# Four output accumulators instead of seven, a ring of 20 weight pairs, and a weight conversion in two steps

## The chip, the cores and the metric

The kernel runs on one core of a Trainium2 chip. The metric is the device time of one execution in microseconds (us). The engines of the core work side by side, each on its own list of instructions in order: TensorE (PE, matrix products), VectorE (DVE), ScalarE (ACT), GpSimd (POOL) and SyncE (SP, which issues all the DMAs here). They wait for one another through semaphores.

## What is computed

Causal attention with a decay gives x (2304 x 512). A gate and two layers follow:

```
logits = x @ w_gate;  P = exp(logits - logits.max())
for _ in range(8):                       # row, then column normalisation
    P /= P.sum(1, keepdims=True) + 1e-09
    P /= P.sum(0, keepdims=True) + 1e-09
    P *= N / E
for e in range(8):                       # 512 -> 1024 -> 512
    out += P[:, e:e+1] * (np.maximum(x @ w1[e], 0) @ w2[e])
h = out @ w_in                           # 512 -> 2048, w_in and w_out are float64
result = np.maximum(0.01 * h, h) @ w_out # 2048 -> 512
```

## The kernel before

**Products.** A fp32 product is made of three TensorE products, since each operand is held as a high and a low part (hi x hi, hi x lo, lo x hi). On top of that each 2 x 2 block product is done with seven products instead of eight (Strassen's form as Winograd wrote it), so its operands are blocks or sums of blocks. Such a product is 12 matmuls of 128 x 384 and takes 2.08 us.

**Units.** The tokens are cut into three parts of 768. The first layer has 16 groups of weights (two for each expert) and the second layer four, g = 16 to 19. A unit u is one group for one part. Part 0 skips the groups 0 to 3: their work is done in small steps ("fills") during the attention and at the start, into the tiles `acc`. So units 0 to 7 are the groups 0 to 3 of parts 1 and 2, units 8 to 43 the rest of the first layer, part by part within a group, and units 44 to 55 the second layer. In unit u's window TensorE does the seven products p1 to p7 of u (into h) and the seven products l1 to l7 of u - 1 (out of h), in the order p1 p2 l1 p6 l2 l6 p7 p5 l5 l7 p3 p4 l3 l4.

**What hangs on it.** From the p products ScalarE copies and VectorE adds the blocks of h (L1048, L1051, L1054) and applies the nonlinearity (L1065). GpSimd makes the sums S1 to S4 of them (L1074), ScalarE the high parts (L1079) and VectorE the low parts (L1083). The l products go to PSUM banks, and `evict` (L1092; L1090 where a sum begins) adds each to one of the part's seven accumulators, P2, C21, P53, P5, K, U2 and U3. Two banks of PSUM serve the l products, x and y. l6 writes the bank that held l1, so it waits for l1's eviction, "e l1"; likewise l5 waits for l2's. After the last group of a layer `x_add` (L1096) makes output blocks out of the accumulators, three additions for each part.

**Weights.** `w_make` splits a block of a group's two matrices (which = 0, first, and 1, second) into a pair of a high part (ScalarE, L161) and a low part (GpSimd, L162). `w_sum` (VectorE, L850) makes the sums of blocks, s0 to s3, in place; s0 comes after the pair 0 of the same matrix is made. There are 14 pairs, each in the place of its own position, and pair i of group g + 1 is made as soon as pair i of g has been used for the last time: those of the first matrix in the window of part 2, those of the second in the window after it.

**Conversion.** w_in and w_out come as float64. The `conv_*` functions turn them into fp32 in 64 pieces of 128 x 256: a load of 256 KB (L890), a square on ScalarE (L894), four operations on VectorE (L899 to L902) and a store (L903). A group of the second layer then loads its weights from there. Two pieces are done in each of the units 8 to 39.

**Operands.** The seven operands b11, b21, t2, t3, t1, b22 and t4 of a part (blocks and sums of blocks of x, high and low) are made once for each layer, go to DRAM, and come back for each product as loads of 768 KB into a ring of four (`xw`, L1014).

**Order.** It is written by hand: `at(time, key, name, function, need=...)` gives each step a planned time and the steps it needs. A step's time is raised to just after those it needs, and all steps are then written out sorted by time. Each engine takes its own in that order, so an instruction that waits holds up all behind it on its engine, and on SP all later DMAs.

```
    Q = "p1 p2 l1 p6 l2 l6 p7 p5 l5 l7 p3 p4 l3 l4".split()
    LACC = dict(l1="K", l6="U2", l7="U3", l4="C21", l5="P5", l3="P53", l2="P2")
        chain = {"l6": "l1", "l7": "l6", "l4": "l7", "l3": "l5", "l5": "l2"}
```

## Time and profile before

| | before |
|---|---|
| median of 3 runs | 2248.01 us (2247.16 to 2252.31) |
| the profiled execution | 2241.45 us |
| its span | 2239.3 us |
| TensorE busy in the span | 2066.7 us, 92% |
| VectorE | 1804.3 us, 81% |
| ScalarE | 1003.5 us, 45% |
| GpSimd | 1164.0 us, 52% |
| mean granted TensorE clock | 0.97 of full speed |

The profile is that of one execution, so times in it add up to 2241.45, not to the median. A wait of TensorE in it carries a "releaser": the step that ended it. Busy shares are means over the span; a stage by itself is read from the windows further down.

### The profile page before, as it was taken

To read this page: it belongs to the slowest core of one execution; us is meant where nothing else is said; L and a number is where in the kernel's file an instruction comes from. 1 tells how busy PE (TensorE), PEld (TensorE's weight loads), DVE (VectorE), ACT (ScalarE), POOL (GpSimd) and SP (SyncE) were. 2 spreads that over 40 slices of the span, in tenths; PEclk is the share of its full clock that TensorE was granted. 3 is DMA by queue.
4 is the path that set the end of the run, shared out by engine and by line. 5 is a ranking of instruction groups with operands and counts; after the bars stand their busy time and mean duration, and the time that the engine had idled before them with its cause. 6 is when DMAs were issued, how large, how long until landed. Compare 5 with 4: busy or idle time off the path is not lost.

```text
span 2239.3 us, 32628 instructions
## 1 busy us (share of the span) xinstructions
PE 2066.7 (92%) x11760; PEld 1996.0 (89%) x11760; DVE 1804.3 (81%) x2238; ACT 1003.5 (45%) x1802; POOL 1164.0 (52%) x728
## 2 busy tenths in 40 slices
...
GB/s 138 169 145 148 140 85 247 376 208 235 234 231 234 216 236 208 260 228 215 227 207 244 205 262 223 225 223 228 224 215 262 216 229 265 267 211 202 227 207 118
DMA packets 153512, 483.66 MB, mean 216 GB/s; under 512 B 16793, under 2 KB 42537, under 8 KB 153353
## 3 DMA queue, kind: packets, MB, share of 16 engines
...
HBM read 425.56 MB, written 51.22 MB: 213 GB/s over the span
## 4 chain that ended last, share of the span: by engine, by line
PE 49%; DVE 19%; issue 6%; POOL 5%; DMA 3%; ACT 2%; SPq 0%; DVEq 0%; POOLq 0%; ACTq 0%
PE x L1027 27%; PE y L1027 21%; DVE hl L1083 4%; DVE cv L899 2%; DVE cv L901 2%; DVE cv L900 2%; POOL wl L162 2%; POOL s L1074 2%; DMA xo_t<-stg 1%; DVE y L1051 1%; DVE u L1054 1%; ACT hh L1079 1%; DVE wr L850 1%; DVE acc_U L1092 1%; POOL k L1074 1%
## 5 line engine op out<-in xcount | busy, mean ns | idle before, releaser
L162 POOL TENSOR_TENSOR wl<-wr,wh 128x512 fp32r<-128x512 f32 x288 | 405.3, 1414 | 401.3 <-ACT wh L161 383.6
L1027 PE MATMUL x<-xw,wh 128*128 128x384 f32 x1792 | 467.1, 342 | 18.2 <-ACT k L1048 10.2
L1027 PE MATMUL x<-hh,wh 128*128 128x384 f32 x896 | 313.1, 349 | 75.5 <-DVE acc_K L1092 32.6
L1027 PE MATMUL y<-xw,wh 128*128 128x384 f32 x1344 | 350.8, 342 | 27.7 <-DVE u L1054 27.7
L1027 PEld LDWEIGHTS x<-xw,wh 128*128 128x128 f32 x1792 | 333.8, 194 | 21.7 <-ACT k L1048 11.1
L1027 PE MATMUL x<-hl,wh 128*128 128x384 f32 x896 | 309.0, 345 | 0.0
L1027 PE MATMUL x<-hh,wl 128*128 128x384 f32 x896 | 308.9, 345 | 0.0
L1027 PE MATMUL x<-xw,wl 128*128 128x384 f32 x896 | 303.9, 339 | 0.0
L1074 POOL TENSOR_TENSOR k<-k,u 128x768 f32<-128x768 f32 x56 | 103.3, 1845 | 366.2 <-DVE u L1065 282.6
L1027 PEld LDWEIGHTS y<-xw,wh 128*128 128x128 f32 x1344 | 246.7, 192 | 35.0 <-DVE u L1054 35.0
L1027 PEld LDWEIGHTS x<-hh,wh 128*128 128x128 f32 x896 | 173.7, 194 | 87.9 <-DVE acc_K L1092 40.7
L1027 PE MATMUL y<-xw,wl 128*128 128x384 f32 x672 | 229.4, 341 | 0.0
L1027 PE MATMUL y<-hh,wl 128*128 128x384 f32 x672 | 225.2, 335 | 0.0
L1027 PE MATMUL y<-hh,wh 128*128 128x384 f32 x672 | 225.2, 335 | 0.0
L1027 PE MATMUL y<-hl,wh 128*128 128x384 f32 x672 | 225.0, 335 | 0.0
L161 ACT ACTIVATE wh<-wr 128x512 fp32r<-128x512 f32 x288 | 177.5, 622 | 95.4 <-PE y L1027 58.3
L1079 ACT ACTIVATE hh<-c 128x768 fp32r<-128x768 f32 x112 | 94.5, 844 | 216.3 <-PE y L1027 104.7
L1048 ACT ACTIVATE u<-x 128x768 f32<-128x768 f32 x112 | 90.8, 811 | 217.8 <-DVE hl L1083 181.2
L1092 DVE TENSOR_TENSOR acc_P<-y,acc_P 128x768 f32<-128x768 f32 x138 | 131.4, 952 | 69.7 <-PE y L1027 69.4
L1079 ACT ACTIVATE hh<-u 128x768 fp32r<-128x768 f32 x112 | 94.9, 847 | 195.6 <-PE y L1027 104.3
L1027 PEld LDWEIGHTS x<-hh,wl 128*128 128x128 f32 x896 | 175.3, 196 | 0.0
L1027 PEld LDWEIGHTS x<-hl,wh 128*128 128x128 f32 x896 | 174.9, 195 | 0.0
...
## 6 DMA issues: line engine op xcount, KB each, us to landing
...
xw<-xo_b SPq DMA_DIRECT2D x168, 768.0 KB
...
```

Source lines behind the costliest of these rows:

```text
L161: nc.scalar.activation(hv, src, AF.Copy)
L162: nc.gpsimd.tensor_tensor(lv, src, f(hv), ALU.subtract)
L850: nc.vector.tensor_tensor(o, x, y, op)
L899: nc.vector.tensor_scalar(a, hi, 0x07FFFFFF, 3, ALU.bitwise_and, ALU.logical_shift_left)
L900: nc.vector.scalar_tensor_tensor(a, lo, 29, a, ALU.logical_shift_right, ALU.bitwise_or)
L901: nc.vector.scalar_tensor_tensor(a, hi, 0xC0000000, a, ALU.bitwise_and, ALU.bitwise_or)
L1027: nc.tensor.matmul(o_, w[:, k, w_], m[:, k, :], start=a and k + y == 0, stop=z and k == 1 and y == 2, skip_group_check=True)
L1048: nc.scalar.activation(ctile(u, name, name, bufs), pview(u, p), AF.Copy)
L1074: nc.gpsimd.tensor_tensor(tmp[u, o], tmp[u, a], tmp[u, b], op)
L1079: nc.scalar.activation(hi, tmp[u, LSRC[l]], AF.Copy)
L1083: nc.vector.tensor_tensor(lo, tmp[u, LSRC[l]], f(hi), ALU.subtract)
L1092: nc.vector.tensor_tensor(a, pview(u, l), a, ALU.add)
```

## The change

- The four accumulators of a part are the output blocks themselves, C11, C12, C21 and C22. l1 and l2 both go to C11, l6 and l3 to C12, l5 and l7 to C22, l4 to C21. The additions of `x_add` are no more. In a first group four evictions copy (ScalarE) and three add (VectorE), where all seven copied.
- The room goes to the weight pairs: one ring of 20, over all groups. Pair n takes the place of pair n - 20. So the first pair of a group's second matrix can be made once p2 of part 2 of the group before is done, and its first matrix's once that group's predecessor has done l2 of part 2. The steps are spread over the three windows of a group; the second matrix's mostly fall into the window of part 2.
- A conversion has a step a (two VectorE operations), the square on ScalarE, and a step b (two more, and the store), planned 6.1 us after a. Its two tiles are halves of the former `acc`. 40 pieces are done in units 9 to 41, one in each, and two in units 10, 15, 20, 25, 30, 35 and 40; 24 pieces are done in units 46 to 50, five in each and four in the last. a waits for the load on VectorE. The load is issued after step b of the piece two before.
- Part 0's operands for the first layer are made in units 5 to 8, one about every 13 us. At the start only part 2's and then part 1's are made.
- The last nine steps of the fills stand between unit 0's products (`f` in `QI`), and p1 and p2 of unit 0 take their operands from SBUF (`NEAR`). The transposes of `acc` into the accumulators move from units 0 and 1 to units 2 and 3. The transpose of the probabilities stands after p1 of unit 0.
- The last unit's sums S1 to S4 are on VectorE.

The core of the diff:

```diff
-XR = 4
+XR, WRING = 4, 20
...
-    wpa = pool("wpa", 4)
+    wpa = pool("wpa", 8)
...
-    wpc = pool("wpc", 3)
+    wpc = pool("wpc", WRING - 11)
...
-    ACC = ("P2", "C21", "P53", "P5", "K", "U2", "U3")
-    accp = []
-    for part in range(NPART):
-        own = ACC[:3] if part == 0 else ACC
-        accp.append({n: accs.tile([P, 2, TB], F32, name=f"acc_{n}_{part}") for n in own})
-    for x, n in enumerate(ACC[3:]):
+    ACC = ("C11", "C12", "C21", "C22")
+    accp = [{n: accs.tile([P, 2, TB], F32, name=f"acc_{n}_{part}")
+             for n in (ACC[:2] if part == 0 else ACC)} for part in range(NPART)]
+    for x, n in enumerate(ACC[2:]):
         accp[0][n] = half(acc_all[:, x * PT:(x + 1) * PT])
-    XPLACE = dict(b11="P2", b12="C21", b21="P53", b22="P5", t1="K", t2="U2", t3="U3", t4="C21")
+    spare = [accs.tile([P, 2, TB], F32, name=f"spare{x}") for x in range(3)]
+    spare += [half(acc_all[:, x * PT:(x + 1) * PT]) for x in (2, 3)]
...
-        pool_ = (wpc if i < 3 else wpa) if which == 0 else (wpa if i < 4 else wpb)
-        W[g, n] = w_split(blk(g, which, WSRC[which][n]), which, pool_)
+        x = (14 * g + 7 * which + i) % WRING
+        W[g, n] = w_split(blk(g, which, WSRC[which][n]), wpc if x < WRING - 11 else wpa if x < WRING - 3 else wpb)
...
+        t = spare[3 + j % 2].rearrange("p k t -> p (k t)")
+        wd = t[:, 0:2 * FH].bitcast(U32)
+        return wd, wd[:, 0::2], wd[:, 1::2], t[:, 2 * FH:3 * FH]
-    def conv_square(j):
-        wd, a, o = conv_tile(j)
-        nc.scalar.activation(o, f(wd[:, 1::2]), AF.Square)
-
-    def conv_bits(j):
-        wd, a, o = conv_tile(j)
-        lo, hi = wd[:, 0::2], wd[:, 1::2]
+    def conv_a(j):
+        _, lo, hi, o = conv_tile(j)
+        a = o.bitcast(U32)
         nc.vector.tensor_scalar(a, hi, 0x07FFFFFF, 3, ALU.bitwise_and, ALU.logical_shift_left)
         nc.vector.scalar_tensor_tensor(a, lo, 29, a, ALU.logical_shift_right, ALU.bitwise_or)
+
+    def conv_square(j):
+        _, lo, hi, o = conv_tile(j)
+        nc.scalar.activation(f(lo), f(hi), AF.Square)
+
+    def conv_b(j):
+        _, lo, hi, o = conv_tile(j)
+        a = o.bitcast(U32)
         nc.vector.scalar_tensor_tensor(a, hi, 0xC0000000, a, ALU.bitwise_and, ALU.bitwise_or)
-        nc.vector.scalar_tensor_tensor(o, o, TINY * TINY, f(a), ALU.is_ge, ALU.mult)
+        nc.vector.scalar_tensor_tensor(o, f(lo), TINY * TINY, o, ALU.is_ge, ALU.mult)
         nc.sync.dma_start(out=conv_src(j)[1], in_=o)
...
-        ps = pw["t"] = bank(ps1, "x1")[:, 0, :]
+        ps = pw["t"] = l2_bank()[:, 0, :]
...
-    INIT = dict(P2=(0, 0), P53=(0, 1), C21=(1, 0), P5=(1, 1))
+    INIT = dict(C11=(0, 0), C12=(0, 1), C21=(1, 0), C22=(1, 1))
...
-    QI = "p1 p2 p6 P2 p7 p5 P53 C21 p3 p4 P5".split()
+    QI = "p1 p2 f f p6 f f p7 p5 f f p3 f p4 f f".split()
...
-    LACC = dict(l1="K", l6="U2", l7="U3", l4="C21", l5="P5", l3="P53", l2="P2")
+    LACC = dict(l1="C11", l2="C11", l6="C12", l3="C12", l5="C22", l7="C22", l4="C21")
...
+    NEAR = ("p1", "p2")
...
-        nc.gpsimd.tensor_tensor(tmp[u, o], tmp[u, a], tmp[u, b], op)
+        (nc.vector if u == NU - 1 else nc.gpsimd).tensor_tensor(tmp[u, o], tmp[u, a], tmp[u, b], op)
...
-        new = g in (0, GE) or part == 0 and g == 4 and LACC[l] not in INIT
-        if new:
+        if g in (0, GE) and l in ("l1", "l6", "l5", "l4"):
             nc.scalar.activation(a, pview(u, l), AF.Copy)
         else:
             nc.vector.tensor_tensor(a, pview(u, l), a, ALU.add)
-    def x_add(stage, part, o, a, b, eng):
-        acc_ = accp[part]
-        eng.tensor_tensor(acc_[o], acc_[a], acc_[b], ALU.add)
...
+    for x, (dur, fns) in enumerate(fills[:nf - 9]):
...
+        xhi[0, 0] = {n: a[0] for n in XOPS}
+        xat[0, 0] = dict(b11=e[0], b12=e[1], t1=e[1], b22=e[0], t2=e[0], b21=e[1], t4=e[1], t3=e[2])
...
+    tp_ = base + 0.5
...
+    TURN = {(2, 0): "C11", (2, 1): "C12", (3, 0): "C21", (3, 1): "C22"}
...
+    t0 = unit0[4] + 2.0
+    st = (unit0[8] - 24.0 - t0) / 7
...
+        ta = t0 + st * x
+        for m, y in load:
+            at(ta - 6.0, X, f"load {n} {m}", lambda m=m, y=y: x_block(0, m, spare[y]), need=last)
+        ld = [(X, f"load {n} {m}") for m, _ in load]
+        if n[0] == "t":
+            at(ta, X, n, *((x_sum3,) if n == "t3" else (x_sum, 0, 0, n, nc.vector)), need=last + ld)
+            ld = [(X, n)]
+        at(ta + 1.1, X, "h " + n, x_hi, 0, 0, n, need=last + ld)
+        lo = spare[4] if n not in ("t4", "t3") else None
+        at(ta + 2.2, X, "l " + n, x_lo, 0, 0, n, nc.vector, lo, need=[(X, "h " + n)])
+        at(ta + 3.3, X, "o " + n, x_out, 0, 0, n, lo, need=[(X, "l " + n)])
+        last = [(X, "o " + n)]
...
+    U2 = keys.index((0, GE))
+    cu = []
+    for u in range(9, U2 - 2):
+        cu += [(u, 0)] + ([(u, 1)] if u % 5 == 0 else [])
+    for u in range(U2 + 2, U2 + 8):
+        cu += [(u, x) for x in range(5)]
+    for j, (u, x) in enumerate(cu[:64]):
+        C = ("cv", j)
+        ta = unit0[u] + (2.2, 8.4, 14.6, 20.0, 26.2)[x]
+        need = [(("cv", j - 2), "b")] if j > 1 else [(("x", 0, 0), "o " + n) for n in XOPS]
+        at(ta - 8.0, C, "load", conv_load, j, need=need)
+        at(ta, C, "a", conv_a, j, need=[(C, "load")])
+        at(ta + 2.0, C, "square", conv_square, j, need=[(C, "a")])
+        at(ta + 6.1, C, "b", conv_b, j, need=[(C, "square")])
...
+        g_, x = divmod(n - WRING, 14)
+        u_, name = keys.index((2, g_)), (PSEQ + LSEQ)[x]
+        return E_[u_, name] + 0.2, [(u_, name)]
...
+            t0, sp_ = unit0[us[0]] + 5.0, SL * len(us)
...
+                tf, need = w_free(14 * g + 7 * which + x)
+                ts.append(max(t0 + sp_ * (7 * which + x), tf, ts[-1] + 0.7 if ts else tf))
+                nd.append(need)
...
+            w_events(None, g, which, ts, [ts[0] + 1.0, ts[0] + 1.8, ts[0] + 2.6, ts[1] + 1.0],
+                     lambda x, nd=nd: nd[x])
...
-    conv_at = {}
-    for u in range(NU):
-        if 4 <= g and len(conv_at) < 64:
-            for x in range(2):
-                conv_at[len(conv_at)] = (u, unit0[u] + (2.2, 14.6)[x])
-    for j, (u, tj) in conv_at.items():
-        C = ("cv", j)
-        need = [(("cv", j - 2), "bits")] if j > 1 else [(("start"), "exp")]
-        at(tj - 10.0, C, "load", conv_load, j, need=need)
-        at(tj - 0.5, C, "square", conv_square, j, need=[(C, "load")])
-        at(tj, C, "bits", conv_bits, j, need=[(C, "square")])
...
-            ts = [e(p) + 0.2 for p in PSEQ]
-            w_events(u, g + 1, 0, ts, [ts[0] + x for x in (6.0, 7.0, 8.0, 9.0)],
...
-            ts = [E_[u, l] + 0.2 for l in LSEQ]
-            w_events(u + 1, g + 1, 1, ts, [ts[0] + x for x in (1.0, 2.0, 3.0, 4.0)],
...
-            for n, o, a, b, l, la in (("b11", "P2", "P2", "K", "l2", "l1"),
-                                      ("b22", "P5", "P5", "U3", "l7", "l5"),
-                                      ("b21", "P53", "P53", "U2", "l3", "l6")):
-                ta = E_[u, l] + 1.2
-                at(ta, X, n, x_add, 1, part, o, a, b, p_, need=[(key, "e " + l), (key, "e " + la)])
...
-            for n, o, a, b, l, la in (("b11", "P2", "P2", "K", "l2", "l1"),
-                                      ("b22", "P5", "P5", "U3", "l7", "l5"),
-                                      ("b21", "P53", "P53", "U2", "l3", "l6")):
-                ta = E_[u, l] + 1.2
-                at(ta, key, "y " + n, x_add, 2, part, o, a, b, nc.vector,
-                   need=[(key, "e " + l), (key, "e " + la)])
```

What stands in a row now is shown at three places. Lines have moved a little: L899 to L902 are now L889, L890, L899 and L900; L1092 is L1095, L1083 is L1087, L850 is L846, L903 is L901 and L890 is L884.

The first place is VectorE in the window of part 2 of a first-layer group. Here cv is the conversion, L1092 adds l1's result out of the bank x to its accumulator ("e l1"), and L850 are the weight sums. Before:

```order
L899 TENSOR_SCALAR cv<-cv 128x256
L900 SCALAR_TENSOR_TENSOR cv<-cv 128x256
L901 SCALAR_TENSOR_TENSOR cv<-cv 128x256
L902 SCALAR_TENSOR_TENSOR cv<-cv 128x256
L1051 TENSOR_TENSOR y_10008<-y_10008,k_10028 128x2x384
L1065 SCALAR_TENSOR_TENSOR k_10028<-y_10008,pb 128x768
L1092 TENSOR_TENSOR acc_K_4924<-x_10038,acc_K_4924 128x768
L1083 TENSOR_TENSOR hl<-u_9817,hh 128x768
L850 TENSOR_TENSOR wr<-wr 128x2x256 x2
L850 TENSOR_TENSOR ws<-wr 128x512
L1092 TENSOR_TENSOR acc_P_1_4920<-y_10079,acc_P_1_4920 128x768
L850 TENSOR_TENSOR wr<-wr,ws 128x2x256
```

After (the conversion's tile is now a half of `acc`):

```order
L889 TENSOR_SCALAR acc<-acc 128x256
L890 SCALAR_TENSOR_TENSOR acc<-acc 128x256
L1055 TENSOR_TENSOR y_9817<-y_9817,k_9834 128x2x384
L1069 SCALAR_TENSOR_TENSOR k_9834<-y_9817,pb 128x768
L846 TENSOR_TENSOR wr<-wr 128x2x256 x2
L1095 TENSOR_TENSOR acc_C_1_4873<-x_9839,acc_C_1_4873 128x768
L846 TENSOR_TENSOR ws<-wr 128x512
L1087 TENSOR_TENSOR hl<-u_9630,hh 128x768
L899 SCALAR_TENSOR_TENSOR acc<-acc 128x256
L900 SCALAR_TENSOR_TENSOR acc<-acc 128x256
L846 TENSOR_TENSOR wr<-wr,ws 128x2x256
L1095 TENSOR_TENSOR acc_C_1_4873<-y_9884,acc_C_1_4873 128x768
```

Half of the conversion moved behind l1's eviction, and the first two weight sums, now those of the second matrix, moved ahead of it.

The second place is VectorE in the window of a unit of the second layer (units 46 to 50). Before:

```order
L1083 TENSOR_TENSOR hl<-c_19055,hh 128x768
L1083 TENSOR_TENSOR hl<-s_19057,hh 128x768
L1051 TENSOR_TENSOR y_19104<-y_19104,k_19119 128x2x384
L1092 TENSOR_TENSOR acc<-x_19121,acc 128x768
L1083 TENSOR_TENSOR hl<-u_18901,hh 128x768
L1092 TENSOR_TENSOR acc_P_0_4917<-y_19155,acc_P_0_4917 128x768
L1083 TENSOR_TENSOR hl<-k_18844,hh 128x768
L1092 TENSOR_TENSOR acc<-x_19121,acc 128x768
L1083 TENSOR_TENSOR hl<-c_19055,hh 128x768
```

After:

```order
L1087 TENSOR_TENSOR hl<-s_18605,hh 128x768
L889 TENSOR_SCALAR acc<-acc 128x256
L890 SCALAR_TENSOR_TENSOR acc<-acc 128x256
L899 SCALAR_TENSOR_TENSOR acc<-acc 128x256
L900 SCALAR_TENSOR_TENSOR acc<-acc 128x256
L1055 TENSOR_TENSOR y_18648<-y_18648,k_18665 128x2x384
L1095 TENSOR_TENSOR acc_C_0_4871<-x_18671,acc_C_0_4871 128x768
L1087 TENSOR_TENSOR hl<-u_18430,hh 128x768
L899 SCALAR_TENSOR_TENSOR acc<-acc 128x256
L900 SCALAR_TENSOR_TENSOR acc<-acc 128x256
L889 TENSOR_SCALAR acc<-acc 128x256
L890 SCALAR_TENSOR_TENSOR acc<-acc 128x256
```

Between the low parts (hl) and the evictions there are now conversion steps, b of one piece right ahead of a of the next.

The third place is SP in units 46 to 50: the loads of operands (xw), of weights (wr), and now of pieces (in_w_in) and the stores of converted ones (wf). Before:

```order
L1014 DMA xw<-xo_0_b_143 128x1536
L1014 DMA xw<-xo_0_t_144 128x1536
L1014 DMA xw<-xo_1_b_145 128x1536
L1014 DMA xw<-xo_1_b_146 128x1536
L1014 DMA xw<-xo_1_t_147 128x1536
L1014 DMA xw<-xo_1_t_148 128x1536
L1014 DMA xw<-xo_1_t_149 128x1536
L1014 DMA xw<-xo_1_b_150 128x1536
L1014 DMA xw<-xo_1_t_151 128x1536
L150 DMA wr<-wf_0_0_168 128x1024
L150 DMA wr<-wf_0_1_169 128x1024
```

After:

```order
L1014 DMA xw<-xo_1_t_144 128x1536
L1014 DMA xw<-xo_1_t_145 128x1536
L901 DMA wf_0_0_169<-acc 128x256
L884 DMA acc<-in_w_in_dram 128x512
L1014 DMA xw<-xo_1_t_146 128x1536
L901 DMA wf_0_0_169<-acc 128x256
L884 DMA acc<-in_w_in_dram 128x512
L1014 DMA xw<-xo_1_b_147 128x1536
L901 DMA wf_0_0_169<-acc 128x256
L884 DMA acc<-in_w_in_dram 128x512
L1014 DMA xw<-xo_1_t_148 128x1536
```

Each store and the piece's load behind it now stand between two loads of operands.

## Rows read from the trace of the kernel before

**Rows 1.** The page's first line.

```profile
span 2239.3 us, 32628 instructions
```

**Rows 2.** Stretches: us; busy PE, PEld, DVE, ACT, POOL; PE clock; DMA share; GB/s.

```profile
329.00:397.94 68.94, 57.50 (x277) 50.14 (x275) 46.09 (x88) 28.57 (x49) 33.40 (x21) 0.93 0.67 235
397.94:482.98 85.04, 56.44 (x278) 54.54 (x277) 51.90 (x44) 34.80 (x50) 46.31 (x27) 0.82 0.77 296
482.98:657.70 174.72, 174.72 (x1010) 174.72 (x1010) 143.57 (x143) 78.37 (x110) 113.52 (x67) 1.00 0.70 241
657.70:1697.68 1039.98, 971.41 (x5377) 955.17 (x5377) 928.93 (x1010) 362.94 (x534) 479.29 (x277) 0.97 0.65 227
...
1785.04:1921.04 136.00, 101.56 (x505) 96.40 (x505) 98.51 (x78) 56.98 (x78) 87.97 (x45) 0.89 0.75 256
1921.04:2183.12 262.08, 262.08 (x1513) 262.08 (x1513) 165.98 (x165) 137.55 (x184) 137.84 (x79) 1.00 0.62 213
```

**Rows 3.** Waits of PE, units 8 to 39: total us, times, longest.

```profile
PE x L1027 <- DVE acc L1092: 25.4, 10, 2.8
PE y L1027 <- DVE u L1054: 21.6, 18, 2.0
```

**Rows 4.** The tile cv: min/median/max ns of each operation, and who waited.

```profile
L899 DVE TENSOR_SCALAR cv<-cv x64: 279/1652/1949, 662.4 to 1683.9; 128x256 uint32<-128x256 uint32 x64
L900 DVE SCALAR_TENSOR_TENSOR cv<-cv x64: 424/910/1409, 664.4 to 1684.2; 128x256 uint32<-128x256 uint32 x64
L901 DVE SCALAR_TENSOR_TENSOR cv<-cv x64: 424/427/1955, 664.8 to 1684.7; 128x256 uint32<-128x256 uint32 x64
L902 DVE SCALAR_TENSOR_TENSOR cv<-cv x64: 424/425/1537, 665.4 to 1685.2; 128x256 f32<-128x256 f32 x64
...
  ACT cv L894: 14.5, 12
```

**Rows 5.** Timeline, unit 22: start us, length us, engine, operation, wait before it.

```profile
1116.90 1.93 DVE L899 TENSOR_SCALAR cv<-cv 128x256 uint32<-128x256 uint32 x1
1118.87 1.39 DVE L900 SCALAR_TENSOR_TENSOR cv<-cv 128x256 uint32<-128x256 uint32 x1
1120.30 1.39 DVE L901 SCALAR_TENSOR_TENSOR cv<-cv 128x256 uint32<-128x256 uint32 x1
...
1125.01 0.44 PE L1027 MATMUL x<-hh,wh 128*128 128x384 f32 x1 [0.65 <-DVE acc_K L1092]
```

**Rows 6.** Timeline: VectorE in unit 40, GpSimd in unit 3.

```profile
1704.12 0.96 DVE L1092 TENSOR_TENSOR acc_K<-x,acc_K 128x768 f32<-128x768 f32 x1
...
517.95 1.84 POOL L1074 TENSOR_TENSOR c<-c,s 128x768 f32<-128x768 f32 x1
519.76 3.25 POOL L162 TENSOR_TENSOR wl<-wr,wh 128x512 fp32r<-128x512 f32 x2
```

**Rows 7.** Weight sums, units 8 to 39: busy us, mean ns | idle before.

```profile
L850 DVE TENSOR_TENSOR wr<-wr 128x512 f32<-128x512 f32 x42 | 28.9, 688 | 0.7
```

**Rows 8.** Timeline: a piece's load is issued, and its square on ScalarE waits for it.

```profile
1222.17 0.38 SPq L890 DMA_DIRECT2D cv<-in_w_in_dram  x1
1229.96 0.44 ACT L894 ACTIVATE cv<-cv 128x256 f32<-128x256 f32 x1 [2.09 <-DMA cv<-in_w_in_dram]
```

**Rows 9.** Timeline, the last unit: the addition of `x_add`, and l1.

```profile
2213.62 2.55 DVE L1096 TENSOR_TENSOR acc_P<-acc_P,acc_U 128x768 f32<-128x768 f32 x1
2217.18 0.66 PE L1027 MATMUL x<-hh,wh 128*128 128x384 f32 x1 [4.35 <-DVE acc_C L1092]
```

**Rows 10.** Waits of PE from 329 to 483 us: total us, times, longest.

```profile
PE x L986 <- ACT acc_P L991: 8.8, 1, 8.8
PE x L953 <- DVE prob L946: 6.1, 1, 6.1
PE y L986 <- ACT acc_P L991: 5.9, 1, 5.9
```

350 lines of the change are left out of this document (197 added, 153 removed).

## The prediction

> **What bounds the kernel now.** I read the profile in four steps.
>
> First the span: 2239.3 us [rows 1], and the execution that left it took 2241.45 us. All sums below are made against that 2241.45. The median of the runs, 2248.01, is 6.6 above it, and 6.6 is added at the end.
>
> Second, the stretches between the starts of the units [rows 2]. A window holds 14 products of 2.08 us on TensorE, so it is 29.12 long when TensorE never waits. In units 2 to 7 TensorE is busy 174.72 of 174.72 = 6 x 29.12, and in units 46 to 54 262.08 of 262.08 = 9 x 29.12: nothing is to be had there. What is lost lies elsewhere. Units 8 to 39 take 1039.98 where 32 x 29.12 = 931.84 would do: 108.1 lost, 3.4 a window. Units 43 to 45 take 136.00 instead of 87.36: 48.6 lost. Units 0 and 1 take 85.04 where 14.56 + 29.12 + 3.3 (24 transposes) = 47.0 would do, 38.0 lost, and before them 11.4 are idle: 49.4 lost.
>
> Third, what ended the waits. In units 8 to 39 TensorE waits nearly always for VectorE: 25.4 us in 10 waits for an accumulation, 21.6 in 18 for the sum into u [rows 3]. These units alone hold the 64 conversions, two a window. The four VectorE operations of one take 0.28 + 0.42 + 0.42 + 0.42 = 1.55 us at their shortest and 1.65 + 0.91 + 0.43 + 0.43 = 3.4 by their medians [rows 4]. In unit 22 the first three stand at 1.93, 1.39 and 1.39 [rows 5], 5.1 with the fourth, and l6 then starts 0.65 late, "released" by the accumulation of l1.
>
> Fourth, why that hurts. l6 writes the bank that this accumulation empties and is due 5 x 2.08 = 10.40 after its window's start. In unit 40, without a conversion, the accumulation starts at 1704.12 [rows 6], 6.44 after the unit's start at 1697.68, and ends at 7.4. VectorE has 3.0 us to spare at that place, plus about 1.2 that it sat idle; a block of 5.1 is more than both.
>
> **The change part by part.**
>
> *A. Units 8 to 41.* A conversion is cut into a (two operations, 1.65 + 0.91 = 2.6 by the medians, 3.3 in unit 22) and b (the other two), with the square between them. An a of 3.3 fits into the 4.2 found above, where a block of 5.1 did not. Most windows also have one conversion instead of two. Against that, the window of part 2 gets the second matrix's pairs, and the sum s0 now stands ahead of the accumulation of l1 on VectorE. s0 waits for GpSimd's first low part of that matrix, which comes behind the S sums. In unit 3 (it starts at 512.10) the last S sum ends at 519.79, and a low part takes 3.25 / 2 = 1.62 [rows 6]: 521.4, 9.3 after the unit's start. Two sums of 0.69 [rows 7] give 10.7 and the accumulation of 0.96 gives 11.7, so l6 is 1.3 late and the window loses some 1.6: 11 windows, 17.6. The other 23 windows lose 0.6 each (0 if the slack holds, 0.9 if a stands at its worst), 13.8. Seven windows hold a second conversion in the middle; such a block costs 21.6 / 18 = 1.2 [rows 3], 8.4. Together 40 of the 108.1 stay: **-68**. Ends: 34 x 0.6 = 20 stay (-88), or 11 x 3.3 + 23 x 0.9 + 8 = 65 stay (-43).
>
> *B. Units 46 to 50 get 24 conversions.* VectorE is busy 165.98 / 9 = 18.4 in a window there [rows 2], so 10.7 are free. Five conversions at 3.4 need 17.0. GpSimd is busy 137.84 / 9 = 15.3 of 29.12, half the window, which puts the price between the two ends as in units 8 to 39, so I take the median. 18.4 + 17.0 + 1.5 for landings (0.3 each) = 36.9, 7.8 over the window: VectorE bounds these windows. Four of them 31.2, and the fifth with four conversions 18.4 + 13.6 + 1.2 - 29.1 = 4.1: **+35**. VectorE now waits itself for the load of a piece (the wait was ScalarE's before), and behind it stand accumulations. A load took 7.8 from issue to use where it was waited for [rows 8]. In a window that VectorE fills, a load follows the b of the piece two before and has a whole fifth of the window, some 7, hence 0.3. Ends: 0 (every operation at its shortest, 18.4 + 7.8 = 26.2, fits), and 5.1 a conversion, (18.4 + 25.5 + 1.5 - 29.1) x 4 + 11 = 76.
>
> *C. Units 43 to 45*, where operands for the second layer are made. One addition on GpSimd per part leaves the chain, 3 x 1.84 (an S sum, [rows 6]) = 5.5; what remains (the sums t1, t2 and t4, the splits, the stores and the loads of operands) is unchanged: **-6**. Ends: -18, if all nine additions stood on the path, +6, if the shared staging places add 2 us of wait to each part.
>
> *D. The end.* l1 of the last unit waits 4.35 us for an accumulation that stands behind the addition of 2.55 which is dropped [rows 9]: **-4**, between -2.5 and -6 with the slower clock after that wait.
>
> *E. The start.* Three of its waits go with what is moved: 8.8 and 5.9 for copies after transposes, and 6.1 for the last step of the probabilities, whose transpose now stands behind a product [rows 10], together 20.8. TensorE is busy 56.44 for 47.0 of work in units 0 and 1, at a granted clock of 0.82 [rows 2], and 9 of these 9.4 I give to the idle time that goes. 24 transposes, 3.3, leave this stretch. The rest of the idle time, some 20 (u0's first results through ScalarE and VectorE), stays: **-33**. Ends: -21 (the waits alone) and -46 (only 3 of 49.4 stay).
>
> *F. Units 2 to 7.* The transposes come here, +3.3. Three windows of part 2 get the sums of A ahead of the accumulation, 3 x 1.6 = 4.8. The first part's operands add 11 VectorE operations of 0.96 and 12 loads and 14 stores on SP between units 5 and 8. VectorE is busy 143.57 / 6 = 23.9 of 29.12 there, and 10.6 over more than three windows lie in that slack; I charge 1: **+9**, between 3 and 18.
>
> The last unit's S sums on VectorE, the unchanged number of evictions (three of seven of a first group are now additions on VectorE instead of copies on ScalarE) and the weight pairs made earlier go at nothing: they lie beside TensorE's products, and if that cover is gone they show as an accumulation waited for, about 1 us each.
>
> **Sum:** -68 + 35 - 6 - 4 - 33 + 9 = -67. 2241.45 - 67 = 2174.5, and with 6.6 **2181**.
>
> **The rivals.**
>
> *Rival 1: the conversions are almost free in the second layer.* VectorE's first operation took 0.28 at its shortest and 1.93 beside GpSimd [rows 4, 5], while the accumulation of l1, which reads a bank of TensorE's, took 0.96 [rows 6]. If a conversion is only long while it waits for GpSimd's instruction to end, that wait overlaps GpSimd's work and is paid once: 7 splits x 0.96 + 8 / 3 weight sums x 0.69 + 5 x 1.55 for VectorE and 15.3 for GpSimd, 31.6 in all. The 15.3 hold GpSimd's own waits too, so B is between 0 and 12 (5 windows x 2.5); with 6 instead of 35 the time is **2152**. For it: the two far ends of the same operation. Against it: the medians, and in units 8 to 39 a window lost 3.4 with just two conversions. By the Trainium skill, "SBUF — State Buffer", section "Who interferes with whom", a VectorE instruction with two inputs in SBUF and a GpSimd instruction that reads SBUF exclude each other for a whole instruction, and which was issued first decides who waits. The two lengths above agree with it, and by it the time would be this rival's.
>
> *Rival 2: the split does not do what it says for the first layer.* The accumulation of l1 is late again, now behind an a of 3.3 and the sums that wait for GpSimd, in every window. At 2.4 a window the 34 windows keep 83 of the 108.1, and A is worth 25: 2181 + 43 = **2224**. For it: the order on VectorE puts two sums, and an a, ahead of that accumulation in the windows of part 2. Against: only every third window has the sums.
>
> *Rival 3, slower: VectorE stalls on each piece of the second layer.* SP issues everything in order. The store of a piece waits there for b, and the load of the next piece and the operands of TensorE (768 KB each) stand behind it. By the plan a load is issued some 4.7 us before its a, and 7.8 are needed [rows 8]: 3.1 of wait on VectorE for each, beside 5.1 of work. (18.4 + 5 x 8.2 - 29.1) x 4 + 22 = 143 for B instead of 35: **2289**. It makes the kernel slower once B passes 67 + 35 = 102, which is 6.5 us of VectorE, work and wait, for each of the 24 conversions; I forecast 3.7. For it: 12 of the 64 loads were waited for before [rows 4]. Against: a VectorE that is late also gives the loads more time.
>
> **How the numbers follow.** The forecast has 0.60; its own range, by the terms' ends taken as independent, is 2150 to 2215. Rival 1 has 0.22, rival 2 0.12 and rival 3 0.06. The range from 2130 to 2230 holds the forecast's case almost wholly, most of rival 1 (its lower part, with A and E at their better ends, falls out) and most of rival 2; what it leaves out is rival 3 and the tails, under 0.2. A measurement of this kernel can't tell less than about 0.3%, 6.7 us, from no change: 2241 to 2255. Below that lie the first three cases, but for 0.02 of rival 2's tail: 0.92 faster. The same: 0.03. Slower, rival 3 but for its lower tail: 0.05.
>
> **What would show each step.** A: windows 8 to 41 of 29.5 to 31.5; those of part 2 the longest, with l6 waiting for the accumulation of l1 and GpSimd's low part ending just before. B: units 46 to 50 of about 37 with VectorE busy nearly throughout; 30 would show rival 1, 55 rival 3, with idle time of VectorE that a DMA ended. C: units 43 to 45 of 41 to 44 each on average. D: no wait of over 2 us at the last unit's l1. E: no more waits of 5 us and over for copies between the last step of the fills and the first unit's end. F: units 2 to 7 near 184. I am wrong at the base if a window of the second layer is longer while VectorE has idle time in it, or if the ring of weight pairs makes TensorE wait for a weight.

## The result and the profile after

The changed kernel takes 2222.11 us (median of 4 runs, 2220.35 to 2222.5), the kernel before 2247.59 (4 runs): a ratio of 0.9888, 95% interval 0.9861 to 0.9915. It is faster by 1.1%, the way that was forecast, and the range held the time. But 67 us were forecast and 25.5 came. The runs of the kernel before spread over 2240.51 to 2252.31 (the later sets of seven, beside e11 to e14, have medians of 2241.86 and 2241.56), so a few of the 25.5 us are their scatter. The profiled execution took 2222.18 us, 19.3 less than that of before, which makes the terms of the sum comparable one by one.

The same stretches of the kernel after, cut at the starts of the same units (0, 2, 8, 43, 46, 51 and 55; the last row is unit 55 and the end). The columns are those of [rows 2].

```profile
329.00:404.35 75.35, 50.12 (x238) 43.06 (x237) 44.28 (x88) 28.42 (x48) 32.59 (x21) 0.86 0.62 220
404.35:474.82 70.47, 57.40 (x292) 53.56 (x292) 48.27 (x44) 25.61 (x41) 38.52 (x23) 0.93 0.62 221
474.82:672.17 197.35, 184.45 (x1034) 181.20 (x1033) 151.59 (x158) 84.97 (x121) 116.28 (x70) 0.97 0.72 252
672.17:1712.29 1040.12, 1007.14 (x5713) 989.82 (x5713) 911.15 (x966) 374.69 (x539) 516.43 (x295) 1.00 0.67 232
1741.41:1877.67 136.26, 100.70 (x505) 96.34 (x505) 92.94 (x82) 53.67 (x74) 73.36 (x39) 0.86 0.72 252
1877.67:2051.51 173.84, 156.28 (x841) 150.98 (x841) 147.94 (x188) 82.69 (x129) 75.00 (x45) 0.96 0.68 233
2051.51:2168.04 116.53, 116.53 (x673) 116.53 (x673) 71.43 (x74) 52.13 (x67) 52.35 (x29) 1.00 0.60 209
2168.04:2220.40 52.36, 45.62 (x253) 45.01 (x252) 32.68 (x35) 15.91 (x19) 4.68 (x2) 0.96 0.35 123
```

From the lengths, against 29.12 for each window and against [rows 2]:

| term | forecast | measured | how |
|---|---|---|---|
| A, units 8 to 41 | -68 | -58.1 | 1040.12 - 34 x 29.12 = 50.0 lost, 108.1 before |
| B, units 46 to 50 | +35 | +28.2 | 173.84 - 5 x 29.12, 0 before |
| C, units 43 to 45 | -6 | +0.3 | 136.26, 136.00 before |
| D, the end | -4 | -3.8 | unit 55 and the end 52.36, 56.18 before |
| E, the start | -33 | -8.2 | unit 2 starts at 474.82, at 482.98 before |
| F, units 2 to 7 | +9 | +22.6 | 197.35, 174.72 before |
| sum | -67 | -19.0 | -19.3 by the two executions |

E alone makes half of the error of 48, F and A most of the rest. The other 6.6 of the forecast, the distance of the median from the profiled execution, did not come again: after, both are the same.

**The start.** Where TensorE idled before unit 0's first product: the timeline from 375 to 401 us, SP, ScalarE, VectorE and TensorE.

```profile
375.20 5.07 SPq L764 DMA_DIRECT2D acc_C<-xd  x8
...
398.24 0.84 ACT L777 ACTIVATE xc<-acc_C 128x768 fp32r<-128x768 f32 x1 [5.65 <-DMA xo_t<-xc]
398.99 0.47 ACT L166 ACTIVATE hh<-x 128x384 fp32r<-128x384 f32 x1
...
399.11 0.96 DVE L781 TENSOR_TENSOR acc_C<-acc_C,xc 128x768 fp32r<-128x768 f32 x1 [6.59 <-ACT xc L777]
399.99 0.55 DVE L167 SCALAR_TENSOR_TENSOR hl<-x,hh 128x384 fp32r<-128x384 f32 x1
...
400.60 3.92 PE L201 MATMUL x<-xp,w 128*128 128x384 f32 x12 [17.80 <-DVE hl L167]
```

L777 and L781 make high and low parts of part 1's operands, L166 and L167 split a result of the fills. All of part 1's operand steps stand in one run on ScalarE and VectorE, right behind the load of its blocks (the first row). The last of them waits 5.65 us for a staging place that a store still reads, and the split that TensorE needs stands behind it. In unit 1 a like thing happens, with a weight of group 1 whose load had been issued 8.8 us before:

```profile
428.61 2.24 SPq L150 DMA_DIRECT2D wr<-in_w_dram  x4
...
437.41 0.63 ACT L161 ACTIVATE w<-wr 128x512 fp32r<-128x512 f32 x1 [10.83 <-DMA wr<-in_w_dram]
...
438.82 0.69 PE L1027 MATMUL x<-hh,w 128*128 128x384 f32 x1 [4.57 <-ACT hh L1083]
```

**Units 2 to 7.** Unit 5, which starts at 569.70: GpSimd's low parts, VectorE's first weight sum and the accumulation of l1 behind it, and l6.

```profile
579.01 1.82 POOL L1078 TENSOR_TENSOR c<-c,s 128x768 f32<-128x768 f32 x1
580.79 2.48 POOL L162 TENSOR_TENSOR w<-wr,w 128x512 fp32r<-128x512 f32 x2
...
583.30 0.69 DVE L846 TENSOR_TENSOR wr<-wr 128x512 f32<-128x512 f32 x1 [5.34 <-POOL w L162]
583.91 0.95 DVE L1095 TENSOR_TENSOR acc_C<-x,acc_C 128x768 f32<-128x768 f32 x1
...
584.91 0.68 PE L1027 MATMUL x<-hh,w 128*128 128x384 f32 x1 [4.54 <-DVE acc_C L1095]
```

The sum waits 5.34 us and holds an accumulation whose product was ready since about 576. Unit 7 has the same with 3.83, unit 3 with 0.95. GpSimd comes late to the weight because its first sum of the unit comes late: that waits for VectorE, which has steps of part 0's operands (L774 and L781) ahead of the nonlinearity (L1069). Of the rows below, the first two are of the kernel after, the others of unit 5 before, which starts at 570.34:

```profile
561.13 0.96 DVE L781 TENSOR_TENSOR acc<-spare,acc 128x768 fp32r<-128x768 f32 x1
568.85 1.85 POOL L1078 TENSOR_TENSOR k<-k,u 128x768 f32<-128x768 f32 x1 [2.76 <-DVE u L1069]
```
```profile
566.33 1.84 POOL L1074 TENSOR_TENSOR k<-k,u 128x768 f32<-128x768 f32 x1 [1.07 <-DVE u L1065]
577.63 3.25 POOL L162 TENSOR_TENSOR wl<-wr,wh 128x512 fp32r<-128x512 f32 x2
```

**Units 8 to 41.** Waits of TensorE in them (total us, times, longest), and unit 15, a window of part 1, which starts at 884.51: step a of its first conversion, the accumulation of l1 and l6. Its second conversion follows behind; weight sums of the second matrix fall into windows of part 2.

```profile
PE x L1027 <- DVE acc_C L1095: 21.8, 26, 1.6
PE y L1027 <- DVE u L1058: 10.8, 14, 2.4
```
```profile
889.87 1.38 DVE L889 TENSOR_SCALAR acc<-acc 128x256 uint32<-128x256 uint32 x1
891.29 1.94 DVE L890 SCALAR_TENSOR_TENSOR acc<-acc 128x256 uint32<-128x256 uint32 x1
...
895.01 0.95 DVE L1095 TENSOR_TENSOR acc_C<-x,acc_C 128x768 f32<-128x768 f32 x1
...
896.02 0.44 PE L1027 MATMUL x<-hh,w 128*128 128x384 f32 x1 [0.94 <-DVE acc_C L1095]
```

The first row of [rows 3] holds part 0's accumulators alone. Those of parts 1 and 2 had this row before:

```profile
PE x L1027 <- DVE acc_K L1092: 19.2, 15, 3.3
```

So 44.6 us in 25 waits for an accumulation became 21.8 in 26, and 21.6 for the sum into u became 10.8. What is left is small but regular: most windows with one conversion lose 0.8 to 1.5 us, whichever part they belong to (three of part 0 lose 2.7, two of part 1 at most 0.5), and those with two lose 1.3 to 5.3.

### The profile page after: what moved, and what is told of

Read it like the earlier page. It is cut to its first block, busy times and chain, and to the rows that moved or that the text cites. A ratio compares the mean times of both kernels' runs of the same rounds, so it can differ in the third digit from the quotient of the medians.

```text
span 2220.4 us, 32472 instructions
## 1 busy us (share of the span) xinstructions
PE 2055.6 (93%) x11760; PEld 1974.8 (89%) x11760; DVE 1779.7 (80%) x2257; ACT 984.0 (44%) x1784; POOL 1124.7 (51%) x709
## 4 chain that ended last, share of the span: by engine, by line
PE 57%; DVE 20%; issue 8%; POOL 7%; DMA 4%; ACT 3%; SPq 1%; POOLq 0%; DVEq 0%; ACTq 0%
PE x L1027 28%; PE y L1027 18%; DVE acc_C L1095 3%; DVE wr L846 3%; PE ps_pv L529 3%; POOL w L162 3%; DVE hl L1087 2%; POOL s L1078 2%; PE ps_m L228 2%; PE ps_t L493 2%; POOL k L1078 1%; PE ps_m L201 1%; DVE u L1069 1%; DVE y L1055 1%; PE ps_s L441 1%
## 5 line engine op out<-in xcount | busy, mean ns | idle before, releaser
L162 POOL TENSOR_TENSOR w<-wr,w 128x512 fp32r<-128x512 f32 x288 | 417.8, 1456 | 457.0 <-ACT w L161 402.1
L1027 PE MATMUL x<-hh,w 128*128 128x384 f32 x1792 | 508.9, 345 | 80.2 <-DVE acc_C L1095 56.4
L1027 PE MATMUL x<-xw,w 128*128 128x384 f32 x2676 | 512.1, 340 | 13.2 <-ACT u L1052 4.5
L1027 PEld LDWEIGHTS x<-xw,w 128*128 128x128 f32 x2676 | 475.1, 191 | 23.2 <-ACT u L1052 10.8
L1027 PEld LDWEIGHTS x<-hh,w 128*128 128x128 f32 x1792 | 336.4, 193 | 95.3 <-DVE acc_C L1095 56.3
L1027 PE MATMUL y<-xw,w 128*128 128x384 f32 x2004 | 379.7, 337 | 18.1 <-DVE u L1058 16.2
L1027 PEld LDWEIGHTS y<-xw,w 128*128 128x128 f32 x2004 | 350.6, 189 | 25.2 <-DVE u L1058 23.0
L1027 PE MATMUL y<-hh,w 128*128 128x384 f32 x1344 | 368.4, 334 | 0.0
L1027 PE MATMUL x<-hl,w 128*128 128x384 f32 x896 | 306.2, 342 | 1.6 <-DVE hl L1087 1.6
L1027 PEld LDWEIGHTS y<-hh,w 128*128 128x128 f32 x1344 | 245.1, 188 | 0.2 <-DVE acc_C L1095 0.2
L1083 ACT ACTIVATE hh<-c 128x768 fp32r<-128x768 f32 x112 | 94.3, 842 | 217.8 <-PE y L1027 101.6
L1095 DVE TENSOR_TENSOR acc_C<-y,acc_C 128x768 f32<-128x768 f32 x148 | 140.6, 950 | 53.2 <-PE y L1027 53.2
L1095 DVE TENSOR_TENSOR acc_C<-x,acc_C 128x768 f32<-128x768 f32 x178 | 168.9, 949 | 9.9 <-PE x L1027 9.3
L1083 ACT ACTIVATE hh<-u 128x768 fp32r<-128x768 f32 x112 | 94.1, 840 | 126.0 <-PE y L1027 108.6
L1087 DVE TENSOR_TENSOR hl<-u,hh 128x768 fp32r<-128x768 f32 x112 | 121.6, 1085 | 32.1 <-ACT hh L1083 32.1
L1087 DVE TENSOR_TENSOR hl<-s,hh 128x768 fp32r<-128x768 f32 x56 | 95.4, 1704 | 59.1 <-ACT hh L1083 58.9
L1087 DVE TENSOR_TENSOR hl<-c,hh 128x768 fp32r<-128x768 f32 x112 | 136.9, 1222 | 4.9 <-ACT hh L1083 2.6
```

The source lines that it names most:

```text
L162: nc.gpsimd.tensor_tensor(lv, src, f(hv), ALU.subtract)
L1027: nc.tensor.matmul(o_, w[:, k, w_], m[:, k, :], start=a and k + y == 0, stop=z and k == 1 and y == 2, skip_group_check=True)
L1083: nc.scalar.activation(hi, tmp[u, LSRC[l]], AF.Copy)
L1087: nc.vector.tensor_tensor(lo, tmp[u, LSRC[l]], f(hi), ALU.subtract)
L1095: nc.vector.tensor_tensor(a, pview(u, l), a, ALU.add)
```

## The experiments

Single runs, but for e13_all and e14_more, beside the changed kernel's 2222.1; the stretches of their traces tell more than their totals. "Lost" is the length above 29.12 a window. The code shows the main lines of each edit; "..." stands for lines left out.

### e1_spread and e2_early: the operand steps at the start

```diff
-    T0X = {2: 1.0, 1: base - 34.0}
+    T0X = {2: 1.0, 1: 35.1}            # e1_spread
```

> The changed kernel, with one number of the order changed: the operands of part 1 for the first layer are planned from 35.1 us on, the time at which their load really becomes possible, so that their 21 steps stand 2.6 us apart on ScalarE and VectorE instead of in one clump right behind the load. Theory 1 (the clump is the cause: the fills' splits stand behind it, and TensorE waited 17.80 us at 400.60): that wait breaks up into smaller ones, since the load still lands late, and unit 2 starts 8 to 12 us before 474.82, at 463 to 467; the whole kernel about 2210 to 2214. Rival (the load of part 1's blocks itself, which lands at 381 to 384, and the chain behind it bound the start wherever the fills stand): under 3 us, unit 2 at 472 to 475, 2219 to 2222.

2238.89 us, 16.7 slower, unit 2 at 492.21. The wait of 17.80 was gone and unit 0 started 19.5 earlier, at 384.89. But then unit 0 waited for operands by way of DRAM: 5.36, 8.18, 4.20 and 2.33 us for loads of `xw`, and 3.88 and 1.63 for its first two. Neither side expected it; nearest is the rival. By these waits the chain of part 1's operands bounds the start, and in one clump it even ends earlier.

```diff
-    T0X = {2: 1.0, 1: base - 34.0}
+    T0X = {2: 1.0, 1: 22.0}
-        pre = [(("x", 0, 2), "o " + n) for n in XOPS] if part == 1 else []
+        pre = []                       # and other staging places for part 1
...
```

> The changed kernel, with part 1's blocks loaded 13 us earlier, without waiting for the stores of part 2's operands, and with staging places of its own (part 2's blocks that are done with), so that neither ScalarE nor VectorE waits for a store there. Theory 1: the 17.80 us wait at 400.60 falls to under 4, unit 2 starts at 455 to 461, the whole kernel at 2203 to 2208. Rival (SP and the transfers of the start are the limit, and the loads put before part 2's stores delay these): unit 2 starts at 468 or later, over 2215.

2221.03 us. The 17.80 fell to 8.39 (a step of the gate behind VectorE's t4, which waited 6.34 for a store), unit 0 started at 397.84, 6.5 earlier, and unit 2 at 475.80, no earlier: the rival's case by its numbers. In between, l1 of unit 0 waited 6.4 us for ScalarE, which waited 15.96 for the weight of group 1.

### e3_w1late and e7_start: the weight of group 1

```diff
+                if g == 1 and not which:
+                    tf = max(tf, ends[-1] + 10.0 + 0.7 * x)
```

> The changed kernel, with the first matrix's pairs of group 1 made from 10 us after the fills' end on instead of right behind the issue of their load. Theory: in unit 1 ScalarE's split of that weight waited 10.83 us for the load, and the high part for l1 behind it, so TensorE waited 4.57 and 1.58 at 438.8 and 441.1, and 3.53 and 1.50 later for the copies behind them. Unit 1 (44.92 us) then takes 31 to 36, the whole kernel 2210 to 2214. Rival (the copies and sums of unit 0 are late anyway): unit 1 over 41, 2218 to 2222.

2217.13 us; unit 1 takes 41.08 instead of 44.92, and unit 2 starts at 473.04. The waits of 4.57 and 1.58 are gone, but the eviction of l1 is next with 2.97. Nearer to the rival.

e7_start is that and e2_early, with t4 later:

```diff
+            if X == ("x", 0, 1) and n == "t4":
+                ta = t0 + 14.0
...
```

> The changed kernel with the earlier load and the own staging places of e2_early (there the sum t4 still waited 6.34 us for a store; here it is made later), and the later pairs of group 1 of e3_w1late. Theory 1 (two obstacles in a row: the operand steps ahead of the fills' splits, then the weight of group 1; taking one away lets the other eat the gain): unit 2 starts at 458 to 467 instead of 474.82, more than the 1.8 of e3 and nothing of e2 together, and the whole kernel takes 2204 to 2214. Rival (unit 0 is bound by operands that go through DRAM, wherever its first product starts): unit 1 starts at 425 or later as in all runs so far, 2215 to 2219.

2223.49 us. Unit 0 started at 390.35, 14 earlier than in the changed kernel, and then one wait took it all:

```profile
416.93 3.54 PE L1031 MATMUL x<-xw,w 128*128 128x384 f32 x10 [20.16 <-DMA xw<-xo_t]
```

This was the experiment's own doing: t4 had been planned later, and t2's low part, which overwrites a block that t4 is made from, then came late for p6. So it decides nothing on the theory; with e1 it shows that unit 0 can hang on operands that go through DRAM.

### e9_order and e11_start: part 1's operands first again

```diff
-    T0X = {2: 1.0, 1: base - 34.0}
-    for part in (2, 1):
+    T0X = {1: 1.0, 2: 36.0}
+    for part in (1, 2):
-    QI = "p1 p2 f f p6 f f p7 p5 f f p3 f p4 f f".split()
+    QI = "f f f f f f f f f p1 p2 p6 p7 p5 p3 p4".split()
...
-    NEAR = ("p1", "p2")
+    NEAR = ()
...
```

> The changed kernel with a part of the change undone: at the start part 1's operands are made first and part 2's second (each spread over the time its load leaves), the last nine fill steps stand ahead of unit 0's products, and these read all operands from DRAM; and the pairs of group 1 later, as in e3_w1late (2217.13). Theory 1, mended after e2 and e7 (what the start loses hangs on the part that unit 0 needs being made last: its steps hold up the fills' splits, or unit 0 its operands): the 17.80 us wait goes and no wait for an operand load over 3 us comes in its place, so unit 2 starts at 450 to 460 instead of 473.04, and the kernel takes 2193 to 2205. Rival (ScalarE and VectorE are too full at the start for two parts' operands, whatever the order): part 2's steps hold up the splits or unit 1 as much, 2212 or more.

2209.5 us, unit 2 at 466.59, between the two cases. No operand of unit 0 was waited for. What came in its place was again a weight: ScalarE waited 12.37 us for group 1's load, VectorE's sums behind it, and

```profile
435.14 2.29 PE L1027 MATMUL x<-xw,w 128*128 128x384 f32 x6 [15.90 <-DVE c L1069]
```

```diff
-                    tf = max(tf, ends[-1] + 10.0 + 0.7 * x)    # as in e9_order
+                    tf = max(tf, base + 32.4 + 0.7 * x)
```

> e9_order once more, with one number mended: there the pairs of group 1 were still planned before their load had landed, since the fills, from whose end they were counted, end earlier in that order (ScalarE waited 12.37 us for that load, VectorE's sums 12.73 behind it, and the first product of unit 1 15.9). Now they are planned 32.4 us after unit 0's planned start. Theory 1 (the start loses its time to steps planned right behind the transfer they need: first part 1's operands, then the weights of group 1): unit 2 starts at 447 to 456, 18 to 28 before the changed kernel's 474.82, and the kernel takes 2192 to 2202. Rival (part 2's operands or the weights hold up unit 0 or 1 by as much as before): unit 2 at 464 or later, 2208 or more.

2209.16 us, unit 2 at 462.68: 12.1 of the 18 to 28 expected, between the two cases. The 15.90 is gone; left are waits of 2.33 and 2.34 for part 2's operands, 2.63 and 1.73 in unit 1, and 4.12 among the fills. The later weight gave 3.9 of the 12.1 (e9 to e11); the other 8.2 came with e9, which moved several things at once (the order of the parts, the places of the fills, the way of unit 0's operands and the weight), and no run divides them.

### e4_sums: the weight sums behind the accumulation

```diff
-            w_events(None, g, which, ts, [ts[0] + 1.0, ts[0] + 1.8, ts[0] + 2.6, ts[1] + 1.0],
+            w_events(None, g, which, ts, [ts[0] + x for x in (3.2, 3.9, 4.6, 5.3)] if which and g else
+                     [ts[0] + 1.0, ts[0] + 1.8, ts[0] + 2.6, ts[1] + 1.0],
```

> The changed kernel, with the weight sums of the second matrices planned 2.2 us later, behind the accumulation of l1 on VectorE instead of ahead of it. Theory 2 (the sums wait for GpSimd and hold that accumulation): the waits of 0.95, 4.54 and 3.83 in units 3, 5 and 7 vanish and units 2 to 7 take 180 to 186 instead of 197.35; units 8 to 41 gain 0 to 4 only, since the windows of part 2 lost no more there than the others (1.4 against 1.3); the whole kernel 2205 to 2212. Rival (the weights are then late, or the low parts behind the sums are): waits of l5 or of a product for a weight take their place, 2218 or more.

2204.16 us, 18 faster. Units 2 to 7 lose 14.8 instead of 22.6, as expected. Units 8 to 41 lose 38.5 instead of 50.0, a gain of 11.5 where 0 to 4 were expected: the windows of part 2 with one conversion now lose 0.0 instead of 1.2. In unit 5 the accumulation now stands at 576.99 and the sums behind it; what is left there is 1.67 for l5:

```profile
576.99 0.95 DVE L1095 TENSOR_TENSOR acc_C<-x,acc_C 128x768 f32<-128x768 f32 x1
...
581.40 2.49 DVE L846 TENSOR_TENSOR wr<-wr 128x512 f32<-128x512 f32 x2 [2.42 <-POOL w L162]
...
586.21 0.45 PE L1027 MATMUL y<-hh,w 128*128 128x384 f32 x1 [1.67 <-DVE acc_C L1095]
```

### e5_slot: the same conversions, later in the window

```diff
-        ta = unit0[u] + (2.2, 8.4, 14.6, 20.0, 26.2)[x]
+        ta = unit0[u] + ((2.2, 8.4, 14.6, 20.0, 26.2) if u > U2 else (14.6, 8.4))[x]
```

> The changed kernel, with the first conversion of units 9 to 41 planned at 14.6 us after the unit's start instead of 2.2. Theory 3 (each window loses 1.2 because step a at 2.2 stands beside GpSimd's sums S1 to S4, takes 1.93 + 1.39 instead of 0.28 + 0.42, and delays the accumulation of l1): units 8 to 41 lose 12 to 25 instead of 50.0, the medians of a fall to about 0.3 and 0.45, and the whole kernel takes 2187 to 2200. Rival (any conversion in a window costs about that, since VectorE has no room; at 14.6 it delays the sum into u, as in the kernel before, 21.6 us in 18 waits): 40 to 55 stay, 2215 to 2225.

2199.19 us: 29.0 lost in units 8 to 41 instead of 50.0. The windows of parts 1 and 2 lose 0 to 0.1 (three of part 2 with a second conversion 1.0), those of part 0 that have a conversion, where weight sums of the first matrix stand at the same place, still 1.9 to 3.0. The first operation of a in units 9 to 41, minimum, median and maximum in ns, of the changed kernel and of e5_slot:

```profile
L889 DVE TENSOR_SCALAR acc<-acc x40: 284/1926/1939, 705.9 to 1687.4; 128x256 uint32<-128x256 uint32 x40
```
```profile
L889 DVE TENSOR_SCALAR acc<-acc x40: 280/286/1380, 715.8 to 1680.1; 128x256 uint32<-128x256 uint32 x40
```

The same 40 instructions, 1926 ns at the median beside GpSimd's sums and 286 away from them. The Trainium skill ("SBUF — State Buffer", section "Who interferes with whom") says that a VectorE instruction in a two-port mode and a GpSimd instruction block each other for a whole instruction, and names tensor_scalar among those that can use that mode; these two rows agree with the blocking, though no row shows the mode. The prediction took that section's rule for two inputs in SBUF, and this operation has one. The second operation of a has two, and it went from 1392 ns at the median to 426.

### e8_first and e10_slots: all conversions in the first layer

```diff
     for u in range(9, U2 - 2):
-        cu += [(u, 0)] + ([(u, 1)] if u % 5 == 0 else [])
-    for u in range(U2 + 2, U2 + 8):
-        cu += [(u, x) for x in range(5)]
+        cu += [(u, 0), (u, 1)]         # at 14.6 and 20.7
...
```

> The changed kernel, with all 64 conversions in the first layer, two in each of units 9 to 40, still in two steps, at 14.6 and 20.7 after the unit's start; none in the second layer. Theory 3: away from GpSimd's sums a split conversion is nearly free, so units 8 to 41 lose 10 to 25 and units 46 to 50 lose 3 to 8, the change of the eviction's first copy alone; the whole kernel 2165 to 2180. Rival (two conversions a window cost what two cost before, 3.4 a window): 100 and more in units 8 to 41, about 2250.

2233.16 us. Units 46 to 50 lose nothing: all of B is the conversions. But units 8 to 41 lose 90.2, nearer to the rival. Step a was short everywhere (285 ns at the median); step b of the second piece, 6.1 us behind its a, fell beside GpSimd's sums, which stand around the start of the next unit, and ahead of two accumulations:

```profile
1082.81 1.42 DVE L899 SCALAR_TENSOR_TENSOR acc<-acc 128x256 uint32<-128x256 uint32 x1
1084.33 1.88 DVE L900 SCALAR_TENSOR_TENSOR acc<-acc 128x256 f32<-128x256 f32 x1
1086.14 0.94 DVE L1095 TENSOR_TENSOR acc_C<-y,acc_C 128x768 f32<-128x768 f32 x1
...
1089.74 0.41 PE L1027 MATMUL x<-hh,w 128*128 128x384 f32 x1 [2.33 <-DVE acc_C L1095]
```

e10_slots, with the sums of e4_sums; b stands 4.1 behind a where that is planned at 20.6:

```diff
+    SLOTS = {0: (18.0,), 1: (9.0, 13.6, 20.6), 2: (10.2, 15.6)}
+    for u in range(9, U2 - 2):
+        cu += [(u, x) for x in SLOTS[keys[u][0]]]
+    cu = [c for c in cu if c[1] != 13.6 or c[0] < 36]
...
```

> The changed kernel, with the sums of the second matrices behind the accumulation of l1 (e4_sums) and all 64 conversions in units 9 to 41, in two steps, at places where neither step falls beside GpSimd's sums S1 to S4 nor beside weight sums: at 18.0 in windows of part 0, 9.0 and 20.6 (in some also 13.6) in those of part 1, 10.2 and 15.6 in those of part 2. Theory 3 (a conversion costs only where a step of it stands beside GpSimd's sums and ahead of an accumulation; e8 lost 2 to 4 a window since step b of the second, at 26.8, did): units 8 to 41 lose 5 to 20, units 46 to 51 nothing, units 2 to 7 about 15, and the kernel takes 2140 to 2160. Rival (two conversions a window are too much for VectorE in any place): 60 or more lost in units 8 to 41, 2190 or more.

2202.3 us, units 8 to 41 lose 65.1: the rival's numbers, but not its reason, since two conversions fit where they stand well. The windows of part 1 with two conversions lose 0.3, with three 1.7, those of part 2 1.9, those of part 0 3.4 with one conversion, because its b stands just ahead of the last nonlinearity of the unit, which the next unit's p1 waits for:

```profile
783.71 1.92 DVE L900 SCALAR_TENSOR_TENSOR acc<-acc 128x256 f32<-128x256 f32 x1
785.56 0.94 DVE L1069 SCALAR_TENSOR_TENSOR c<-x,pb 128x768 f32<-128x768 f32 x1
...
786.56 0.44 PE L1027 MATMUL x<-xw,w 128*128 128x384 f32 x1 [2.46 <-DVE c L1069]
```

### e6_layer2: the second layer's conversions spread

```diff
-        cu += [(u, x) for x in range(5)]
+        cu += [(u, x) for x in ((4, 0, 1, 2, 3) if u in (U2 + 3, U2 + 4) else range(4))]
-        ta = unit0[u] + (2.2, 8.4, 14.6, 20.0, 26.2)[x]
+        ta = unit0[u] + ((8.4, 14.6, 20.0, 26.2, 2.2) if u > U2 else (2.2, 8.4))[x]
```

> The changed kernel, with the 24 conversions of the second layer spread over units 46 to 51, four in a unit (five in 47 and 48), and mostly away from the sums of GpSimd (at 8.4, 14.6, 20.0 and 26.2 after the unit's start; at 2.2 in two units only). Theory 4 (the conversions there cost about 1.6 us each, VectorE has room for them, and the 28.2 us lost in units 46 to 50 come from the step at 2.2 beside GpSimd's sums and from a that waits for its load): units 46 to 51 lose 8 to 16 instead of 28.3, the whole kernel 2208 to 2214. Rival (VectorE is full, as forecast): 24 conversions cost the same wherever they stand, 24 to 34 lost, 2218 to 2226.

2219.7 us; units 46 to 52 lose 27.2 (201.05 - 6 x 29.12 = 26.3 to unit 51, and 0.9): the rival's case. With four or five pieces in a unit, one b always falls beside the sums (26.2 + 6.1 is 3.2 into the next window), and some a wait for their load (5 times, 5.0 us in all).

### e12_mix, e13_all and e14_more: places chosen by the trace

```diff
+    SLOTS = {0: (), 1: (9.0, 13.6, 20.6), 2: (14.6,)}      # by part; with e4_sums
+    for u in range(9, U2 - 2):
+        cu += [(u, x) for x in SLOTS[keys[u][0]] if x != 13.6 or u < 30]
...
```

> The changed kernel, with the sums behind the accumulation of l1 (e4_sums), no conversion in the windows of part 0, one at 14.6 in those of part 2, two (in seven windows three) at 9.0, 13.6 and 20.6 in those of part 1, and 24 in units 46 to 50 as in the changed kernel. Theory 3 (what a conversion costs is set by what stands beside and behind it, e10 lost 3.4 in each window of part 0, 1.9 in each of part 2 with two, and 0.3 in those of part 1 with two): units 8 to 41 lose 10 to 22 instead of 50.0, units 2 to 7 about 15, units 46 to 50 27; the kernel takes 2176 to 2190. Rival (the places don't matter, only the number): 35 or more in units 8 to 41, 2200.

2167.95 us. Units 8 to 41 lose 4.9 instead of 50.0, with the same 40 conversions: better than expected (the sums of e4 alone left 38.5, the later places of e5 alone 29.0). TensorE is busy there practically without a break:

```profile
663.87:1658.89 995.02, 994.84 (x5713) 989.24 (x5713) 878.76 (x968) 380.96 (x540) 525.70 (x298) 1.00 0.70 243
```

> e11_start and e12_mix in one kernel. If the terms of the start, of the sums and of the places of conversions are independent, as in the sum of the prediction, it takes the changed kernel's 2222.1 less what e11 and e12 gain: 2148 to 2170. If one of them only passes its gain on to another wait, it stays above 2185.

2153.84 us (2149.44 to 2154.95, 4 runs), a ratio of 0.9598 to the kernel before, interval 0.9578 to 0.9618. e11 gained 13.0 and e12 54.2, together 67.2; e13 gained 68.3. These two gains add up. It is the fastest kernel of the study.

```diff
-    SLOTS = {0: (), 1: (9.0, 13.6, 20.6), 2: (14.6,)}
+    SLOTS = {0: (), 1: (9.0, 13.6, 20.6), 2: (14.6, 20.6)}
...
-    for u in range(U2 + 2, U2 + 8):
-        cu += [(u, x) for x in (2.2, 8.4, 14.6, 20.0, 26.2)]
+    for u in range(U2 + 2, U2 + 7):
+        cu += [(u, x) for x in (9.0, 15.2)]
```

> e13_all with more of the conversions in the first layer: three in each window of part 1 (9.0, 13.6, 20.6), two in each of part 2 (14.6 and 20.6), none in those of part 0, 55 in all, and the last 9 in units 46 to 50, at most two in a unit, at 9.0 and 15.2. Theory 4, mended after e6 (which lost as much as the changed kernel with four or five a unit: in the second layer the five conversions take VectorE's spare time and put a step beside GpSimd's sums wherever they stand; two a unit fit): units 46 to 50 lose 0 to 8 instead of 27.4, units 8 to 41 between 5 and 15, and the kernel takes 2127 to 2142. Rival (each piece of the second layer costs 1.2 us there, and each further piece in the first layer as much): units 46 to 50 lose 10 or more and units 8 to 41 some 20, 2150 or more.

2165.27 us (4 runs; 0.9665 of before, interval 0.9648 to 0.9682), slower than e13_all and in time the rival's case, but for the second layer the theory's: units 46 to 50 with two conversions a unit lose 2.8 instead of 27.4. Their row, of e14_more and of e13_all:

```profile
1842.99:1991.39 148.40, 146.73 (x841) 145.52 (x841) 110.71 (x129) 80.19 (x114) 78.62 (x46) 1.00 0.67 237
```
```profile
1809.50:1982.45 172.95, 152.66 (x841) 146.47 (x840) 147.32 (x188) 82.53 (x129) 74.76 (x45) 0.99 0.67 234
```

But units 8 to 41 lose 36.3: the second piece in the windows of part 2 has its b where that of part 0 had it in e10_slots, ahead of the nonlinearity that the next p1 waits for, and costs 2.5 a window.

## Why the prediction was right and wrong

**E, the step that failed.** I took three waits, 20.8 us, as gone, let the other idle time stay as it was, and put part 1's operands, which are now made last, at nothing. The three waits did go. New ones took their place: 17.80 before unit 0, and 4.57, 3.53, 1.58 and 1.50 in unit 1. So TensorE's idle time from 329 us to the start of unit 2 fell by 1.7 and not by 20.8, from 40.0 to 38.3 us (lengths less busy times of the first two stretches), and its busy time there by 6.4, from 113.9 to 107.5, where 12.3 were given (9 for the clock, 3.3 for transposes). Part 1's operands were planned for the time at which their load was first allowed; the load was held back to after part 2's last store, and their steps then stood right behind it: seven high parts (L777) in a row on ScalarE from 380.93 to 398.24, where part 2's have other work between. The 17.80 us is not the only limit. e1 removed it and e2 halved it, and unit 2 came no earlier; e7 and e9 removed it too. What each met next was operands through DRAM or a weight planned right behind its load. With both out of the way (e11) 12.1 of the 24.8 us missing are gained; e13_all reaches 459.74 for unit 2. What would have given the other 10 stays open.

**F.** Three windows of part 2 at 1.6 were forecast, by the price worked out for A, and 1 us for part 0's operands. The three lost 4.2, 6.5 and 7.0. In unit 3, without operand steps, GpSimd comes to the second matrix's first pair at 512.56, 7.3 after the unit's start (I had 7.7), and the accumulation costs a wait of 0.95. In unit 5 it comes there only at 580.79, 11.1 after, though in unit 5 before, with the same steps between its sums, it was there at 577.63, 7.3 after. Its first sum starts 0.85 before the unit in the one and 4.01 before it in the other. Part 0's operand steps, which run from unit 4 on and not from 5, stand on VectorE ahead of what that sum waits for. So the term that was too small is the 1 us charged for them. That they are what makes VectorE late is read from the trace; no run moved them. e4 shows the other half: moving four numbers, so that the accumulation no longer stands behind the sums, gave back 7.8 here. The remaining 14.8 hold 3.3 of transposes; how the rest divides was not tried.

**A, right in mechanism, wrong in the slack.** The split did what was forecast, and 50.0 stays where 40 was expected. But I gave step a a room of 4.2 us, read in unit 40, which has no conversion and is a window of part 2. There GpSimd's sums start 3.9 us before the unit does, in most windows of part 1 only some 1.6 before. Unit 15 and unit 16, of part 2, which starts at 914.89:

```profile
882.89 1.85 POOL L1078 TENSOR_TENSOR k<-k,u 128x768 f32<-128x768 f32 x1 [4.50 <-DVE u L1069]
910.96 1.84 POOL L1078 TENSOR_TENSOR k<-k,u 128x768 f32<-128x768 f32 x1 [14.65 <-DVE u L1069]
...
917.99 1.93 DVE L889 TENSOR_SCALAR acc<-acc 128x256 uint32<-128x256 uint32 x1
```

In unit 15 the low part ahead of a waits 1.74 us for ScalarE's high part, and this for GpSimd's sum; a starts 5.4 after the unit's start, and its 3.3 us make l6 0.94 late. In unit 16 a starts 3.1 after, and a and the weight sums together are too much: with either moved away (e5, e4) the windows of part 2 with one conversion lose 0.0. So the losses are alike from unlike causes: medians of 1.0, 1.3 and 1.2 for parts 0, 1 and 2, where 0.6 and, for part 2, 1.6 were forecast. The longest windows are units 20 and 35, 32.9 and 34.4, of part 0 and with two conversions; the sign was that those of part 2 would be. How much of the 50 was due to places is shown in steps: the conversions' place alone gave 21.0 (e5), that of the sums alone 11.5 (e4), and both with places chosen by the trace 45.1 (e12).

**B, right in size, for a reason that was half right.** 28.2 against 35. Without conversions these five windows hold 92.65 us of VectorE's work (e8) and with 24 of them 147.94, so one costs 2.3, not 3.4 (the forecast) and not 1.55 (rival 1). VectorE is busy 29.6 us for each window of 34.8: it has a little more to do than the 29.12 of a window, as forecast, but it idles 25.9 us in the five, above all behind ScalarE's high parts (11.2) and GpSimd's low parts of weights (7.4). A window that is longer while VectorE has idle time was my sign of being wrong at the base, so its work alone is not the bound. It seldom waits for a load: 5.1 us in 7 waits. e6 moved the places and kept the number, and the loss stayed; e14, with two a unit at other places, lost almost nothing. Together they point to the number; no run had two a unit at the old places. Rival 1's blocking shows in the single instruction (e5), and yet its time did not come; rival 2's time came (2224; its 34 windows at 2.4 make 81.6 and not 83), but for another reason, since the split did help; rival 3's waits for loads were small.

**C.** The additions left the chain and nothing was gained. In unit 45 TensorE waits 12.12 us for an eviction that stands on ScalarE behind two operand steps, one that waited 7.99 for VectorE and one that waited 4.18 for a shared staging place. The kernel before had waits of 6.7 at most (the first row is its):

```profile
PE x L1027 <- DVE acc_K L1092: 13.3, 2, 6.7
```
```profile
1847.48 0.84 ACT L777 ACTIVATE acc<-spare 128x768 fp32r<-128x768 f32 x1 [7.99 <-DVE acc_C L781]
...
1854.22 0.84 ACT L777 ACTIVATE acc<-spare 128x768 fp32r<-128x768 f32 x1 [4.18 <-DMA xo_b<-acc]
...
1856.54 0.69 PE L1027 MATMUL x<-hh,w 128*128 128x384 f32 x1 [12.12 <-ACT acc_C L1093]
```

The staging places were the worse end of this term in the prediction. That the operand steps took what the additions gave is read from the trace; no run tried it.

**D** came out as worked out, 3.8 for 4; a wait of 2.2 at l1 is left, where none of over 2 was the sign.

**The range.** The terms' ends, taken as independent (the root of the sum of their squares), give 2137 to 2233 for the forecast's case, not 2150 to 2215; the measured time lies in the first and not in the second.
